# Retention and rational FFN on one core: the value branch of steps 8 to 20 as |b1·h| on ScalarE and one VectorE operation

## The chip, the cores and the metric

The kernel runs on one core of a Trainium2 chip. The metric is the device time of one execution in microseconds (us). Of one execution there is also a profile, which lists every instruction of the engines: TensorE (PE, with its weight loads as PEld), VectorE (DVE), ScalarE (ACT), GpSimd (POOL) and the DMA queues.

## The reference

A retention layer (attention with a decay in place of a softmax) over 8 batches, 8 heads, 576 positions and 64 columns gives 4608 rows of 512. They go through a feed-forward layer of 2048 inner columns whose activation is a ratio of polynomials, element by element:

```
h = x @ w_in
P = a[0] + a[1]*h + a[2]*h**2 + a[3]*h**3
Q = 1 + abs(b[0])*abs(h) + abs(b[1])*h**2
out = (P / (Q + 1e-6)) @ w_out
```

a holds four numbers and b two, and they are known only at run time. Everything is float32.

## The kernel before

**Tiling.** The 4608 rows are nine blocks b of 512 rows, the 2048 inner columns sixteen strips f of 128. A step is one pair (b, f). `gemm1` makes h of a step, a 128x512 tile in PSUM, from 12 matmuls (x and the weights are each split in a high and a low part). The functions `ffn_*` make g = P/Q from it. `gemm2` multiplies g by w_out and adds into the sums of the block, 12 matmuls again. The runs are: steps 0 to 7 (block 0, first half of the strips), steps 8 to 23 (block 1), steps 24 to 31 (block 0, second half), then the other blocks. `gemm2` follows `gemm1` by four steps in steps 8 to 21, by three in most others.

**Early steps.** The weights come from HBM packed as 64-bit words. Until step 23 each strip of weights is loaded and taken apart by `split_weight`: two ScalarE activations (c and bits), one VectorE operation on c, then a ScalarE copy into w and a subtraction on VectorE or GpSimd. `STARTS` says how many splits begin in each step; for steps 8 to 20 it is 0 0 1 1 1 1 1 2 1 0 2 2 1.

**Order.** Each engine gets its instructions in program order (`InOrder`) and runs its queue in that order. In steps 8 to 20 the program order is the list `MID`: start gemm1 split1 ffn_p ffn_hi ffn_r ffn_p2 gemm2 ffn_va ffn_lo split2 ffn_q ffn_v ffn_q3 split3 split0. With i for the step, ScalarE's queue in a step is therefore: c and bits of new splits, p(i) and u(i) from h(i) (`ffn_p`), g(i-2), the logarithm and the exponential that make 1/Q of step i-1 in the tile u (`ffn_r`), v(i) where `VA` says "act" (`ffn_va`), and w of splits that end. VectorE's queue: the operation on c, p·h (`ffn_p`), (p+a1)·h (`ffn_p2`, the last reader of h), v(i) where `VA` says "vector", the two operations of `ffn_q` for step i-1, v·u (`ffn_v`), `ffn_q3` for step i-1, the subtraction of a split.

**Buffers.** h has two PSUM banks (`ps_h`), so gemm1 of step i+2 writes over h(i) and waits for its last reader. In steps 8 to 20 u is not in SBUF but in one of two PSUM banks, `free_at`, which the attention does not need there; from step 21 on it is in SBUF again. v has two buffers, p three. In step 11 the sums of block 0 are taken out of PSUM by two ScalarE copies (o<-acc), and the first `gemm2` of block 1 in step 12 needs the banks that they free.

**The value branch.** Q − (1 + 1e-6) = (|b1|·|h| + |b0|)·|h| is made as u = |h| (ScalarE, in `ffn_p`), v = b1·u + b0 (`ffn_va`: ScalarE or VectorE by the list `VA`), v = v·u (`ffn_v`, VectorE). absb holds |b0| and |b1|, so b0 and b1 in the code are not negative. In steps 8 to 20 `VA` has ScalarE for steps 8, 15 and 16 and VectorE for the ten others.

Of the kernel before, what the change touches and what calls it, by code (L numbers as in the profile page):

```python
# [17 lines left out]
AF = mybir.ActivationFunctionType  # L18
ALU = mybir.AluOpType
# [46 lines left out]
FIRST_DENSE = 22  # L66
SCALES = "scalar pool pool vector pool vector pool scalar pool".split()
SCALES_Q = "vector vector vector pool pool vector vector pool pool".split()
VA = "act act act act vector act act vector act vector vector vector vector vector vector act act vector vector vector vector act act act".split()
LO = "vector pool pool pool pool pool pool pool pool pool pool pool pool vector vector pool pool pool pool pool pool pool vector pool".split()  # L70
WLO = "vector pool pool pool pool pool pool vector vector pool vector vector vector vector pool pool vector vector pool vector pool vector pool vector pool vector pool pool pool pool vector pool".split()
VISITS |= {24 + 2 * i: (8 + i, 9 + i) for i in range(3)}
# [17 lines left out]
def retention_ffn(ctx: ExitStack, tc: tile.TileContext, qkv, w_in, w_out, consts, masks, out):  # L90
# [26 lines left out]
    pe, act, dve, pool = (InOrder(tc, e) for e in (nc.tensor, nc.scalar, nc.vector, nc.gpsimd))  # L117
# [37 lines left out]
    a0, a1, a2, a3 = (ab_sb[:, i : i + 1] for i in range(4))  # L155
    b0, b1 = absb[:, 0:1], absb[:, 1:2]
# [314 lines left out]
    hs = {}  # L471
    els = {}
# [29 lines left out]
        dve.tensor_tensor(p, p, h, ALU.mult)  # L502

    def ffn_p2(b, f):
        p = els[b, f][2]
        dve.scalar_tensor_tensor(p, p, a1, hs.pop((b, f)), ALU.add, ALU.mult)

    def ffn_va(b, f):

        u, v, p = els[b, f]  # L510
        if VA[at[b, f] : at[b, f] + 1] == ["vector"]:
            dve.tensor_scalar(v, u, b1, b0, ALU.mult, ALU.add)
        else:
            act.activation(v, u, AF.Identity, bias=b0, scale=b1)

    def ffn_v(b, f):
        u, v, p = els[b, f]
        dve.tensor_tensor(v, v, u, ALU.mult)

    def ffn_r(b, f):  # L520

# [125 lines left out]
    at = {s[:2]: i for i, s in enumerate(steps)}  # L647
# [84 lines left out]
    for i in range(len(steps) + lag(len(steps))):  # L732
        step = i
        this, prev, prev2 = (steps[j][:2] if 0 <= j < len(steps) else None for j in (i, i - 1, i - 2))
        todo = {"gemm2": (products, i), "start": (split_start, int(STARTS[i]) if i < first else 0)}

        if i in VISITS:
            a, k = VISITS[i]
            todo["visit"] = visit, a, k
            if a is not None:  # L740
                todo |= {f.__name__: (f, a) for f in (keep_hi, keep_lo)}
            if k is not None:
                todo |= {f.__name__: (f, k) for f in ((decay, decay1, add, fade) if a is not None else (decay, add, fade))}
        if i + 1 in VISITS and VISITS[i + 1][1] is not None:
            todo |= {f.__name__: (f, VISITS[i + 1][1]) for f in (scale_q, scale_v)}
        if this:
            todo |= {f.__name__: (f, *this) for f in (gemm1, ffn_p, ffn_p2, ffn_va, ffn_v)}
        if prev:
            todo |= {f.__name__: (f, *prev) for f in (ffn_r, ffn_q, ffn_q3)}
        if prev2:  # L750
            todo |= {"ffn_hi": (ffn_hi, *prev2), "ffn_lo": (ffn_lo, *prev2, i - 2 < first and LO[i - 2] == "pool")}
        if i == half:
            ps = ps_at.tile([P, 2, 512], F32, tag="at", name="free_at")
            free_at.extend((ps[:, 0], ps[:, 1]))
        elif i == FIRST_DENSE - 1:
            free_at.clear()
        whole = i in VISITS
        early = None if half <= i < FIRST_DENSE - 1 or i >= first else (FIRST0, FIRST1, FIRST2, FIRST3, FIRST4, FIRST5, FIRST6, FIRST7, FIRST21, FIRST22, FIRST23)[i if i < half else i - 13]
        dense = DENSE if whole else DENSE_ALONE
        run(END if not this else LAST if i == len(steps) - 1 else MID if free_at else early if i < first else dense if i < 2 * NF else REST, todo)  # L760
        load_weights(2)
# [42 lines left out]
```

## Time and profile before

| | |
|---|---|
| time, median of 3 runs | 869.66 us (868.0 to 869.73) |
| the profiled execution's own time | 868.11 us |
| its span, first to last instruction | 866.0 us |
| PE, DVE, ACT, POOL busy | 98%, 88%, 77%, 15% of the span |
| the chain that ended last, by engine | PE 79%, ACT 10%, DVE 7%, issue 3%, DMA 1% |

The span is what the profile sees; the profiled execution took 2.1 us more than it. A timeline row gives the start of an instruction in us from the span's start, its duration in us, engine, line, operation, output and inputs; in square brackets stands the idle time of the engine just before it and whose end released it. Nearly every instruction is recorded by a helper, line 86, so rows are told apart by their tiles. The steps are told apart by counting h: the h of step 8 is the first whose u goes to free_at.

### The profile page before, as it was taken

The numbers are of one execution on the slowest core, as the hardware profiler recorded it, in microseconds if no ns is written. First come the engines' busy times: TensorE is split into PE (matmuls) and PEld (weight loads), VectorE is DVE, ScalarE is ACT, GpSimd is POOL, SyncE is SP. The second block draws the span as 40 slices with busy tenths as digits, with TensorE's granted clock in tenths as the row PEclk, the third lists the DMA queues.
The fourth block names the chain that finished last, engine by engine and source line by source line (L and its number), as shares of the span: only waits on it lengthen the run. The fifth ranks groups of instructions, "written<-read, shape, count | busy, mean of one in ns | idle before, by whom it ended". The sixth has DMA issues, their size and how long they took to land.

```text
span 866.0 us, 18735 instructions
## 1 busy us (share of the span) xinstructions
PE 845.3 (98%) x7574; PEld 726.4 (84%) x7574; DVE 765.6 (88%) x1221; ACT 669.6 (77%) x1240; POOL 131.2 (15%) x107
## 2 busy tenths in 40 slices
PE   8899899999999999999999999999999999999997
PEld 7667788788888888888888888888888888888886
DVE  5999999999889988898889888888888988888995
ACT  4898999988767778777877787778877787767775
POOL 2522323721001111111111110001111111000000
PEclk9999999999999999999999999999999999999999
DMA  9994000033021112111211121111211121001001
GB/s 345 342 372 178 1 2 0 2 113 116 30 88 50 49 50 98 50 50 50 98 50 51 49 98 51 48 48 31 82 40 50 50 99 50 1 2 48 1 1 48
DMA packets 20774, 64.55 MB, mean 75 GB/s; under 512 B 2512, under 2 KB 2640, under 8 KB 20688
## 3 DMA queue, kind: packets, MB, share of 16 engines
q1 hardware_dynamic: 20528, 63.10, 20.6%
q8 instruction: 59, 0.97, 0.5%
q14 instruction: 27, 0.22, 0.1%
q10 hardware_dynamic: 160, 0.26, 0.1%
HBM read 53.91 MB, written 9.44 MB: 73 GB/s over the span
## 4 chain that ended last, share of the span: by engine, by line
PE 79%; ACT 10%; DVE 7%; issue 3%; DMA 1%; SPq 0%; POOL 0%; POOLq 0%; ACTq 0%; DVEq 0%
PE acc L86 36%; PE h L86 36%; PE ps L86 4%; DVE p L86 3%; PE y L86 2%; DVE v L86 2%; ACT c L86 2%; ACT free_at L86 2%; ACT w L86 1%; ACT p L86 1%; ACT u L86 1%; ACT g L86 1%; DMA qk<-in_qkv 1%; DVE c L86 1%; ACT bits L86 1%
## 5 line engine op out<-in xcount | busy, mean ns | idle before, releaser
L86 PE MATMUL acc<-w,g 128*128 128x512 f32 x1584 | 369.0, 383 | 4.5 <-ACT o L86 2.9
L86 PE MATMUL h<-xhi,w 128*128 128x512 f32 x1152 | 367.2, 381 | 3.6 <-DVE kv L86 1.6
L86 PEld LDWEIGHTS acc<-w,g 128*128 128x128 f32 x1584 | 297.6, 190 | 50.2 <-ACT o L86 3.3
L86 PEld LDWEIGHTS h<-xhi,w 128*128 128x128 f32 x1152 | 217.7, 189 | 37.2 <-ACT c L86 1.7
L86 ACT ACTIVATE p<-h,const_sb 128x512 f32<-128x512 f32 x144 | 111.4, 774 | 161.2 <-PE h L86 154.4
L86 PE MATMUL h<-xlo,w 128*128 128x512 f32 x576 | 218.4, 379 | 0.2 <-DVE xlo L86 0.2
L86 DVE TENSOR_TENSOR p<-p,h 128x512 f32<-128x512 f32 x144 | 98.7, 686 | 47.3 <-ACT u L86 44.9
L86 PEld LDWEIGHTS h<-xlo,w 128*128 128x128 f32 x576 | 108.9, 189 | 16.5 <-issue 0.7
L86 DVE SCALAR_TENSOR_TENSOR p<-p,const_sb,h 128x512 f32<-128x512 f32 x144 | 107.4, 746 | 4.0
L86 ACT ACTIVATE v<-u,absb 128x512 f32<-128x512 f32 x129 | 103.3, 801 | 0.4 <-DVE p L86 0.2
L86 DVE SCALAR_TENSOR_TENSOR p<-v,p 128x512 f32<-128x512 f32 x140 | 98.7, 705 | 3.3
L86 DVE SCALAR_TENSOR_TENSOR p<-p,const_sb,u 128x512 f32<-128x512 f32 x131 | 99.4, 759 | 1.5 <-ACT u L86 1.5
L86 POOL TENSOR_TENSOR S<-S,const_sb 128x256 f32<-128x256 f32 x32 | 32.7, 1022 | 447.6 <-DVE S L86 427.4
L86 DVE TENSOR_TENSOR v<-v,u 128x512 f32<-128x512 f32 x131 | 97.3, 742 | 0.2 <-ACT v L86 0.2
L86 DVE SCALAR_TENSOR_TENSOR v<-v,u 128x512 f32<-128x512 f32 x131 | 89.7, 684 | 0.0
L86 ACT ACTIVATE u<-u 128x512 f32<-128x512 f32 x131 | 82.6, 630 | 4.2
L86 ACT ACTIVATE g<-p 128x512 fp32r<-128x512 f32 x132 | 82.6, 626 | 3.5 <-DVE p L86 3.2
L86 ACT ACTIVATE u<-v 128x512 f32<-128x512 f32 x131 | 81.9, 625 | 1.4 <-DVE v L86 1.4
L86 DVE TENSOR_TENSOR g<-p,g 128x512 fp32r<-128x512 f32 x115 | 78.7, 684 | 0.7 <-ACT g L86 0.7
L86 ACT ACTIVATE u<-h 128x512 f32<-128x512 f32 x131 | 76.8, 586 | 2.0 <-DVE v L86 2.0
L86 ACT ACTIVATE kv<-kv,const_sb 128x64 f32<-128x64 f32 x232 | 58.2, 333 | 4.9 <-DMA kv<-in_qkv 4.9
L86 POOL TENSOR_TENSOR qk<-qk,const_sb 128x512 f32<-128x512 f32 x31 | 44.7, 1442 | 41.0 <-DMA qk<-in_qkv 41.0
(93 smaller groups left out, 699.9 us busy)
## 6 DMA issues: line engine op xcount, KB each, us to landing
qk<-in_qkv SPq DMA_DIRECT2D x36, 512.0 KB, 4.2
kv<-in_qkv SPq DMA_DIRECT2D x32, 512.0 KB, 5.4
bits<-in_w_in SPq DMA_DIRECT2D x16, 512.0 KB, 9.3
bits<-in_w_out SPq DMA_DIRECT2D x16, 512.0 KB, 7.4
out<-o SPq DMA_DIRECT2D x28, 256.0 KB, 3.8
kv<-in_qkv SPq DMA_DIRECT2D x4, 256.0 KB, 6.6
out<-o SPq DMA_DIRECT2D x8, 128.0 KB, 2.1
out<-last SPq DMA_DIRECT2D x2, 256.0 KB, 2.4
```

What stands on the lines that cost most here:

```text
L86: return lambda *a, **k: self.tc.keep_in_program_order(method(*a, **k))
```

## The change

In steps 8 to 20 `VA` now says "abs". There `ffn_p2` also issues, behind its VectorE operation, a ScalarE activation v = |b1·h| that reads h in PSUM; `ffn_va` does nothing; and `ffn_v` is one VectorE operation (v + b0)·u in place of v·u. The list `MID` and all other lists stay as they are.

```diff
-VA = "act act act act vector act act vector act vector vector vector vector vector vector act act vector vector vector vector act act act".split()
+VA = "act act act act vector act act vector abs abs abs abs abs abs abs abs abs abs abs abs abs act act act".split()
     def ffn_p2(b, f):
-        p = els[b, f][2]
-        dve.scalar_tensor_tensor(p, p, a1, hs.pop((b, f)), ALU.add, ALU.mult)
+        u, v, p = els[b, f]
+        h = hs.pop((b, f))
+        dve.scalar_tensor_tensor(p, p, a1, h, ALU.add, ALU.mult)
+        if VA[at[b, f] : at[b, f] + 1] == ["abs"]:
+            act.activation(v, h, AF.Abs, scale=b1)
     def ffn_va(b, f):
         u, v, p = els[b, f]
+        if VA[at[b, f] : at[b, f] + 1] == ["abs"]:
+            return
     def ffn_v(b, f):
         u, v, p = els[b, f]
-        dve.tensor_tensor(v, v, u, ALU.mult)
+        if VA[at[b, f] : at[b, f] + 1] == ["abs"]:
+            dve.scalar_tensor_tensor(v, v, b0, u, ALU.add, ALU.mult)
+        else:
+            dve.tensor_tensor(v, v, u, ALU.mult)
```

## Rows read from the trace of the kernel before

**Rows 1.** The page, part 1: busy time of each engine over the span.
```profile
PE 845.3 (98%) x7574; PEld 726.4 (84%) x7574; DVE 765.6 (88%) x1221; ACT 669.6 (77%) x1240; POOL 131.2 (15%) x107
```

**Rows 2.** Busy time by stretch; columns us, PE, PEld, DVE, ACT, POOL, clock, DMA.
```profile
80.00:160.00 80.00, 75.11 (x337) 64.08 (x335) 77.17 (x120) 76.36 (x121) 26.44 (x20) 0.98 0.00 1
160.00:190.00 30.00, 29.17 (x395) 24.30 (x394) 29.83 (x43) 26.68 (x55) 15.29 (x12) 1.00 0.16 53
190.00:240.00 50.00, 50.00 (x570) 43.50 (x569) 45.89 (x79) 40.46 (x83) 5.58 (x6) 1.00 0.28 94
```

**Rows 3.** Timeline of PE, 97 to 163 us: first matmuls behind its waits.
```profile
100.71 4.54 PE L86 MATMUL acc<-w,g 128*128 128x512 f32 x12 [2.90 <-ACT o L86]
...
112.86 2.75 PE L86 MATMUL acc<-w,g 128*128 128x512 f32 x12
...
147.75 0.48 PE L86 MATMUL h<-xhi,w 128*128 128x512 f32 x1 [0.64 <-DVE p L86]
...
154.40 0.45 PE L86 MATMUL h<-xhi,w 128*128 128x512 f32 x1 [1.20 <-ACT free_at L86]
...
157.06 5.73 PE L86 MATMUL acc<-w,g 128*128 128x512 f32 x24
```

**Rows 4.** Instructions by form, 80 to 160 us: count, busy us, mean ns, idle.
```profile
L86 ACT ACTIVATE p<-h,const_sb 128x512 f32<-128x512 f32 x14 | 10.7, 766 | 0.0
...
L86 DVE SCALAR_TENSOR_TENSOR p<-p,const_sb,free_at 128x512 f32<-128x512 f32 x13 | 9.6, 739 | 0.4 <-ACT v L86 0.3
...
L86 DVE TENSOR_TENSOR v<-v,free_at 128x512 f32<-128x512 f32 x13 | 8.8, 680 | 0.0
...
L86 DVE TENSOR_SCALAR v<-free_at,absb 128x512 f32<-128x512 f32 x10 | 8.1, 807 | 0.4
...
L86 ACT ACTIVATE free_at<-h 128x512 f32<-128x512 f32 x13 | 7.7, 589 | 0.8 <-DVE v L86 0.8
```

**Rows 5.** Timeline of ACT, 84 to 155 us, steps 8 to 20.
```profile
84.04 0.77 ACT L86 ACTIVATE v<-free_at,absb 128x512 f32<-128x512 f32 x1
84.71 0.86 ACT L86 ACTIVATE w<-held 128x512 fp32r<-128x512 f32 x1
...
88.40 0.89 ACT L86 ACTIVATE w<-held 128x512 fp32r<-128x512 f32 x1
...
105.57 0.58 ACT L86 ACTIVATE free_at<-free_at 128x512 f32<-128x512 f32 x1
106.07 0.62 ACT L86 ACTIVATE w<-c 128x512 fp32r<-128x512 f32 x1
...
114.64 0.58 ACT L86 ACTIVATE free_at<-h 128x512 f32<-128x512 f32 x1 [0.52 <-DVE v L86]
...
132.30 0.58 ACT L86 ACTIVATE free_at<-h 128x512 f32<-128x512 f32 x1 [0.30 <-DVE v L86]
133.27 0.64 ACT L86 ACTIVATE g<-p 128x512 fp32r<-128x512 f32 x1 [0.39 <-DVE p L86]
...
134.91 0.62 ACT L86 ACTIVATE w<-c 128x512 fp32r<-128x512 f32 x1
...
154.19 1.14 ACT L86 ACTIVATE w<-c 128x512 fp32r<-128x512 f32 x2
```

**Rows 6.** Timeline of DVE, 88 to 136 us: the two operations on h.
```profile
88.72 0.75 DVE L86 SCALAR_TENSOR_TENSOR p<-p,const_sb,h 128x512 f32<-128x512 f32 x1
...
104.61 0.69 DVE L86 TENSOR_TENSOR p<-p,h 128x512 f32<-128x512 f32 x1 [0.30 <-ACT free_at L86]
105.34 0.75 DVE L86 SCALAR_TENSOR_TENSOR p<-p,const_sb,h 128x512 f32<-128x512 f32 x1
...
135.07 0.75 DVE L86 SCALAR_TENSOR_TENSOR p<-p,const_sb,h 128x512 f32<-128x512 f32 x1
```

**Rows 7.** All waits, summed by pair: us in total, times, longest.
```profile
DVE p L86 <- ACT u L86: 46.4, 82, 1.7
```

**Rows 8.** Busy time and granted clock in short stretches; columns as in rows 2.
```profile
101.00:104.00 3.00, 3.00 (x8) 2.34 (x8) 3.00 (x6) 2.97 (x6) 0.00 (x0) 0.50 0.00 0
...
152.00:155.00 3.00, 1.80 (x9) 1.30 (x8) 2.90 (x5) 2.97 (x7) 1.38 (x2) 1.00 0.00 0
```

## The prediction

> **What bounds the kernel now.** The page comes first: PE is busy for 98% of the span, and no other engine comes near it [rows 1]. So only what makes PE stand still can move the time. The busy time by stretch tells where it does [rows 2]. From 190 us on PE has no gap worth naming (50.00 of 50 in the stretch shown), so a delay that PE has at 190 us is a delay of the end, us for us. Between 80 and 160 us, which holds steps 8 to 20, PE idles 4.89 us, and there both other engines are nearly full: VectorE idles 2.83 us of the 80 and ScalarE 3.64. The change moves work between just these two, in just this stretch.
>
> PE's timeline shows where its gaps lie [rows 3]. Step 12 loses 2.90 us because the two ScalarE copies that empty the sums of block 0 come late; then the matmuls of steps 21 and 22 wait 0.64 and 1.20 us for their bank of h. A step of PE needs 2.59 us for each of its two sets (twelve matmuls take 2.75 with a tail of 0.16), 5.18 in all. ScalarE needs about as much for a step with one split and more with two, so PE runs ahead until it lacks a bank. From 154.40 on, where the h of step 22 starts, PE sets the pace. **The question is thus when that matmul starts.**
>
> One more view matters: who may read h when. In step 12 VectorE's p·h starts at 104.61 after 0.30 of idle [rows 6]. Of its inputs p had long been written; what had just ended is u, which ScalarE also reads from h. Over the whole run VectorE loses 46.4 us in 82 such waits [rows 7]. So two engines do not read one bank of h at a time here: the later one in program order waits. The Trainium skill (PSUM — Partial Sum Buffer, "PSUM bank collisions raise a hardware error") says that reads of one bank by two engines collide, and that semaphores have to keep them apart; the trace agrees with these 46.4 us.
>
> **The change part by part.** VectorE, in ten steps, loses an operation of 0.807 us; in thirteen, v·u of 0.680 becomes a two-scalar-and-tensor form, for which the nearest row has 0.739 [rows 4]. That is 10 × 0.807 − 13 × 0.059 = 7.3 us less for VectorE.
>
> ScalarE gets ten more activations. None that reads h with a scale from a tile and no bias is in the trace. From below it is bounded by u, 0.589, with neither, from above by p, 0.766, with both [rows 4]; it has one of the two, so I take the middle, 0.68. The next instruction starts 0.10 before such a one ends (84.04 + 0.77 against 84.71) [rows 5], so its place in the queue costs 0.58 (bounds 0.49 and 0.67). In steps 8, 15 and 16 it replaces one of 0.67 and saves 0.09.
>
> The Trainium skill (ScalarE: Activation LUTs, "Rules for kernel authors") speaks against this trade: additions and products belong on VectorE, which it calls up to three times as fast. It says so of bf16, and no row here has that form; by that ratio an operation of 0.807 would cost 2.4 us on ScalarE, an estimate, and ten of them some 18 us more than in my sum. The rows of float32 from PSUM have 0.807 against at most 0.766, so the trade is one for one.
>
> The second part is a **new wait**. The activation reads h behind (p+a1)·h in program order, so ScalarE now waits for VectorE to end that. Behind it on ScalarE stand w, the next split's c and bits and then p and u of the next step, for which VectorE and, through the bank, PE wait. How long it is depends on how late VectorE is:
> - Step 12, the common case: ScalarE would be free at 106.07, VectorE is done at 105.34 + 0.75, and 0.04 passes between dependent instructions [rows 5, 6]: 0.06 us.
> - Step 9: ScalarE would be free at 88.40, VectorE only ends at 88.72 + 0.75 = 89.47, with the longer v·u of step 8 at 89.53. The activation starts at 89.57 and ScalarE goes on at 90.15. VectorE has no relief before, since step 8 had its value branch on ScalarE already.
> - Step 17: ScalarE free at 134.91, VectorE done at 135.07 + 0.75. That is 0.95; VectorE loses some 0.25 of its lag in the steps ahead, so I take 0.70. Here too steps 15 and 16 bring VectorE no relief.
>
> The lag of ScalarE's queue against before, summed up:
> - behind step 9: 90.15 − 88.40 = 1.75 (step 8's saving is in it)
> - steps 10 to 14: 5 × (0.58 + 0.06) = 3.20; the 0.52 that it idled in step 14 for VectorE [rows 5] goes: 4.43
> - steps 15 and 16: 2 × (0.06 − 0.09): 4.37
> - step 17: 0.58 + 0.70: 5.65
> - steps 18 to 20: 3 × 0.64 = 1.92: 7.57.
>
> The copies out of the sums in step 11 are late with it, by some 3 us, so the gap of 2.90 grows. That does not count twice: behind it PE again runs ahead of ScalarE. The activation of step 20 is now the last reader of its h. It stands just ahead of the w at 154.19 [rows 5], so it starts at 154.19 + 7.57 − 0.58 = 161.18, ends at 161.86, and the h of step 22 starts at 161.90 and not at 154.40: **7.5 us late**.
>
> What comes back behind it: the 24 matmuls at 157.06 took 5.73 [rows 3]; at 0.215 each and the length of one, 0.38, they need 23 × 0.215 + 0.38 = 5.33. The 0.4 is a wait in the middle for g's low part, which is no longer late when PE is: 7.1. Of the 0.83 that PE idles between 160 and 190 [rows 2], where VectorE is full, I give back 0.2, as VectorE comes there a little less late than PE. That leaves **6.9 us**.
>
> The profiled execution took 868.1 us, so the sum is 875.0. The median of the runs is 1.5 above that execution; from it the sum would be 876.6. I name the middle, 875.8. By the bounds of the activation alone (10 × 0.09 each way) it is 874.9 to 876.7.
>
> **The rivals.**
> - *No wait between the two readers of h.* If VectorE and ScalarE may read h together, the 1.17 of step 9, the 0.70 of step 17 and the 0.06s go, and with them the idle 0.30 and 0.39 of step 17 [rows 5] that ScalarE could fill. The lag behind step 20 is 10 × 0.58 − 3 × 0.09 − 0.52 − 0.69 = 4.3, and after the same 0.6 comes back 3.7: 871.8 to 873.4. Rows 7 speak against it.
> - *The clock falls at the new gaps.* After the 2.90 gap the clock stood at 1.2 of 2.4 GHz, 0.50 from 101 to 104 us, and the twelve matmuls took 4.54 for 2.75; over the gap of 1.20 it stayed at 1.00 [rows 3, 8]. Steps 20 to 22 now have gaps of some 2 us each, in between. If it falls at step 22, 1.8 us more are lost where nothing hides them: 877.6. It decides from a gap somewhere between 1.20 and 2.90.
> - *VectorE was the bound, and this is faster.* By the busy time it is a little fuller than ScalarE [rows 2], and the gaps of 0.64 and 1.20 end with a VectorE operation on h. If its 7.3 us of relief are what counts, both gaps go: 868.1 − 1.8 = 866.3, on the median 867.8. The Trainium skill (VectorE: DVE Perf Modes, "Rules for kernel authors") has it that VectorE's operation count is what to bring down, and by that rule this is the result. It decides if the new activation fits in ScalarE's idle time, 3.64 over ten, 0.36 us each. The cheapest reader of h takes 0.49 of its queue, so I think little of it.
> - *Hidden.* ScalarE's lag could be made up by waits that I count as staying, within 0.2% (1.7 us).
>
> **How the numbers follow.** Forecast 0.63, no wait 0.14, clock 0.11, faster 0.07, hidden 0.05. About 0.2% is what a measurement of this kernel can tell from no change. The first three are slower by more than that: 0.88. The range leaves out faster and hidden, starts at the no-wait case from the profiled time, 871.8, and ends at the clock case with the dear activation, counted from the median, 879.
>
> **What would show it.** ScalarE rows v<-h,absb, thirteen, of 0.59 to 0.77 us; no TENSOR_SCALAR on free_at; a wait of ScalarE's v for VectorE's p of about 1 us in steps 9 and 17 and of a few hundredths elsewhere; ScalarE over 98% busy or waiting in the stretch and VectorE with some 7 us more idle; the copies out of the sums near 102.5; the first matmul of step 22 near 162, and from there the same timeline. I am wrong if ScalarE's v starts while VectorE still reads h, if its other activations get shorter when VectorE does less, or if PE starts step 22 before 157.

## The result, and the profile after

The kernel after takes 875.13 us (median of 4 runs, 874.57 to 876.18); the kernel before, run beside it, took 869.59 (4 runs, 868.00 to 869.73). The ratio of the runs is 1.0076 [1.0064, 1.0089], some 6.6 us slower; the two medians lie 5.5 us apart. The forecast was 875.8, between 871.8 and 879.0. The profiled execution of after took 875.41 us with a span of 873.3; that of before took 868.11 with 866.0.

The page, part 1, of after (busy time of each engine, its share of the span, instructions), beside [rows 1]:
```profile
PE 847.7 (97%) x7574; PEld 727.4 (83%) x7574; DVE 762.7 (87%) x1211; ACT 675.8 (77%) x1250; POOL 132.9 (15%) x107
```
VectorE lost 2.9 us of work and ScalarE got 6.2, and the time followed neither share: on the page both engines look three quarters or more full, as before. Where the time went stands in the busy time by stretch, beside [rows 2]; after's stretches are cut 7 us later, so that they hold the same work (us, PE, PEld, DVE, ACT, POOL, clock, DMA):
```profile
80.00:160.00 80.00, 71.57 (x311) 59.91 (x310) 68.23 (x100) 75.25 (x120) 21.62 (x16) 0.96 0.00 1
160.00:167.00 7.00, 5.26 (x25) 4.28 (x24) 6.76 (x9) 6.91 (x14) 4.98 (x4) 1.00 0.01 2
167.00:197.00 30.00, 29.55 (x397) 24.89 (x396) 29.82 (x43) 26.87 (x54) 15.60 (x12) 1.00 0.16 51
197.00:247.00 50.00, 50.00 (x570) 43.50 (x569) 45.91 (x79) 40.78 (x84) 5.57 (x6) 1.00 0.27 93
```
From 167 us on, PE's busy time is within 0.4 us of what it was from 160 us on before, stretch by stretch. All that was lost is lost ahead of that. VectorE now idles 12 us of the first 80 instead of 3, while ScalarE idles 5 instead of 4.

PE's timeline, 97 to 171 us, beside [rows 3] (start, us, what, and in brackets the idle time before it with its releaser):
```profile
103.83 5.49 PE L86 MATMUL acc<-w,g 128*128 128x512 f32 x12 [3.84 <-ACT o L86]
...
141.12 0.48 PE L86 MATMUL h<-xhi,w 128*128 128x512 f32 x1 [0.61 <-ACT v L86]
...
148.47 0.48 PE L86 MATMUL h<-xhi,w 128*128 128x512 f32 x1 [1.90 <-ACT v L86]
...
155.16 0.48 PE L86 MATMUL h<-xhi,w 128*128 128x512 f32 x1 [1.25 <-ACT v L86]
...
162.35 0.48 PE L86 MATMUL h<-xhi,w 128*128 128x512 f32 x1 [1.74 <-ACT v L86]
...
165.04 5.34 PE L86 MATMUL acc<-w,g 128*128 128x512 f32 x24
```
The h of step 22 starts at 162.35 instead of 154.40. The releaser of all four waits for h is now the new activation v: it has become the last reader of the bank. The 24 matmuls behind it take 5.34 where they took 5.73.

Of those 7.95 us, 0.50 was there before the change begins. That shows in ScalarE's p of step 8, the first operation on the h of that step. In the ScalarE timeline of before it stands at
```profile
81.16 0.76 ACT L86 ACTIVATE p<-h,const_sb 128x512 f32<-128x512 f32 x1
```
and in that of after, with the waits that matter beside [rows 5]:
```profile
81.66 0.76 ACT L86 ACTIVATE p<-h,const_sb 128x512 f32<-128x512 f32 x1
...
90.07 0.69 ACT L86 ACTIVATE v<-h,absb 128x512 f32<-128x512 f32 x1 [1.01 <-DVE p L86]
...
102.76 1.93 ACT L86 ACTIVATE o<-acc 128x1024 f32<-128x1024 f32 x2
...
128.38 0.69 ACT L86 ACTIVATE v<-h,absb 128x512 f32<-128x512 f32 x1 [0.33 <-DVE p L86]
...
137.80 0.63 ACT L86 ACTIVATE g<-p 128x512 fp32r<-128x512 f32 x1 [0.57 <-DVE p L86]
...
140.38 0.69 ACT L86 ACTIVATE v<-h,absb 128x512 f32<-128x512 f32 x1 [0.85 <-DVE p L86]
...
161.61 0.69 ACT L86 ACTIVATE v<-h,absb 128x512 f32<-128x512 f32 x1
```
So each kernel is best measured by one stretch, **from step 8's p to the first matmul of step 22**: 73.24 us before, 80.69 after, 7.45 more. What follows that matmul took 711.6 us of the span before and 710.95 after. It was between 710.95 and 713.4 in every kernel below, so this stretch carries nearly all of the difference, but for e1 and e8 to e10, where up to 1.8 us more is lost behind it.

The two VectorE operations that the waits of 1.01 and 0.85 end with, beside [rows 6]:
```profile
89.29 0.75 DVE L86 SCALAR_TENSOR_TENSOR p<-p,const_sb,h 128x512 f32<-128x512 f32 x1
...
139.60 0.75 DVE L86 SCALAR_TENSOR_TENSOR p<-p,const_sb,h 128x512 f32<-128x512 f32 x1
```
89.29 + 0.75 = 90.04, and v starts at 90.07; 139.60 + 0.75 = 140.35, and v starts at 140.38. The two readers of one bank do follow each other.

The forms, 80 to 167 us, beside [rows 4] (count, busy us, mean ns, idle before them):
```profile
L86 DVE SCALAR_TENSOR_TENSOR p<-v,p 128x512 f32<-128x512 f32 x14 | 12.1, 867 | 0.0
...
L86 DVE SCALAR_TENSOR_TENSOR v<-v,absb,free_at 128x512 f32<-128x512 f32 x13 | 9.6, 742 | 0.0
L86 DVE TENSOR_TENSOR p<-p,h 128x512 f32<-128x512 f32 x14 | 9.6, 688 | 10.2 <-ACT free_at L86 10.2
...
L86 ACT ACTIVATE v<-h,absb 128x512 f32<-128x512 f32 x13 | 8.9, 687 | 2.2 <-DVE p L86 2.2
```
The new activation takes 0.687 us (0.68 forecast), the new VectorE operation 0.742 (0.739). VectorE now waits 10.2 us for ScalarE ahead of p·h, 1.4 before: what it was relieved of became waiting for the engine that was given more.

### The profile page after: what moved, and what is told of

The parts are those of the page before. It is cut to its first block, busy times and chain, and to the rows that moved or that the text cites. A ratio compares the mean times of both kernels' runs of the same rounds, so it can differ in the third digit from the quotient of the medians.

```text
span 873.3 us, 18733 instructions
## 1 busy us (share of the span) xinstructions
PE 847.7 (97%) x7574; PEld 727.4 (83%) x7574; DVE 762.7 (87%) x1211; ACT 675.8 (77%) x1250; POOL 132.9 (15%) x107
## 4 chain that ended last, share of the span: by engine, by line
PE 76%; DVE 3%; ACT 2%; issue 0%; POOL 0%; SPq 0%; POOLq 0%; ACTq 0%
PE acc L86 36%; PE h L86 34%; PE ps L86 4%; PE y L86 2%; DVE p L86 1%; DVE v L86 1%; ACT free_at L86 0%; DVE c L86 0%; ACT g L86 0%; ACT p L86 0%; ACT kv L86 0%; ACT c L86 0%; ACT w L86 0%; POOL g L86 0%; DVE qk L86 0%
## 5 line engine op out<-in xcount | busy, mean ns | idle before, releaser
L86 POOL TENSOR_TENSOR S<-S,const_sb 128x256 f32<-128x256 f32 x32 | 35.7, 1116 | 448.8 <-DVE S L86 425.1
L86 POOL TENSOR_TENSOR qk<-qk,const_sb 128x512 f32<-128x512 f32 x31 | 42.4, 1368 | 38.9 <-DMA qk<-in_qkv 38.9
```

Of the source, the lines that this page charges most:

```text
L86: return lambda *a, **k: self.tc.keep_in_program_order(method(*a, **k))
```

## The experiments

The theory is that ScalarE's queue is what the stretch goes by, and that ten activations and ScalarE's new wait for VectorE are paid there in full. The rivals are that VectorE set the pace, that the place of the activation is what costs, and that the idle times of ScalarE are slack to be filled. All figures of the stretch are the one defined above, less 73.24, and come from one profiled execution each; the two timing columns are medians and ratios to the kernel before, run beside each.

| kernel | stretch, us | span, us | time, us | ratio |
|---|---|---|---|---|
| before | 0 | 866.0 | 868.48 to 869.59 | 1 |
| after: all of 8 to 20 | +7.45 | 873.3 | 875.13 | 1.0076 [1.0064, 1.0089] |
| e3_abs_three: 8, 15, 16 | +0.08 | 866.0 | 868.08 | 0.9995 [0.9984, 1.0006] |
| e5_abs_9_11: 9 to 11 | +2.80 | 868.7 | 871.63 | 1.0035 [1.0023, 1.0046] |
| e6_abs_17_20: 17 to 20 | +2.81 | 868.3 | 871.64 | 1.0035 [1.0022, 1.0048] |
| e11_abs_9: step 9 | +1.34 | 867.7 | 869.82 | 1.0012 [1.0003, 1.0021] |
| e12_abs_18: step 18 | +0.61 | 867.3 | 869.21 | 1.0002 [0.9990, 1.0015] |
| e4_vector_less | −0.87 | 865.3 | 867.50 | 0.9990 [0.9978, 1.0002] |
| e7_scalar_less | +1.39 | 867.7 | 870.07 | 1.0013 [1.0003, 1.0022] |
| e1_act_all | +6.10 | 873.3 | 875.21 | 1.0080 [1.0065, 1.0095] |
| e2_abs_early | +5.48 | 871.5 | 874.03 | 1.0069 [1.0054, 1.0084] |
| e8_w_vector | +7.76 | 876.5 | 875.66 | 1.0072 [1.0055, 1.0089] |
| e9_early_w_vector | +5.00 | 872.5 | 874.34 | 1.0067 [1.0045, 1.0089] |
| e10_before_w_vector | +5.10 | 873.2 | 875.25 | 1.0073 [1.0054, 1.0093] |

### Is it VectorE? The product left out

```diff
     def ffn_v(b, f):
         u, v, p = els[b, f]
+        if at[b, f] in (9, 10, 11, 12, 13, 14, 17, 18, 19, 20):
+            return
         dve.tensor_tensor(v, v, u, ALU.mult)
```


> Edit: from the kernel before, the ten steps with the branch on VectorE leave out the product v*u, so VectorE has 10 x 0.60 us less of its queue and ScalarE nothing more (Q lacks a factor |h| there). Queue theory: ScalarE sets the pace; it gets back at most its idle time for VectorE, 0.52 in step 14 and 0.69 in step 17, so 0.5 to 1.6 us faster than before. Rival, VectorE is the bound of the stretch: the gaps of PE at steps 21 and 22 go and more, 2 to 6 us faster.

VectorE's busy time on the page falls by 5.4 us (765.6 to 760.2), more than the 2.9 of the change, and ScalarE is given nothing: the stretch shortens by 0.87 us, the span by 0.7, and the time by an amount that its interval does not set apart from none. PE's gap at step 22 in this run:
```profile
153.66 0.45 PE L86 MATMUL h<-xhi,w 128*128 128x512 f32 x1 [1.16 <-ACT free_at L86]
```
The gap of 1.20 is 1.16, with the same releaser. The rival "VectorE was the bound" falls. The rule put beside it, that VectorE's operation count is what to bring down (Trainium skill, VectorE: DVE Perf Modes, "Rules for kernel authors"), does not give the time here: ten operations less shortened the stretch by 0.87 us.

### Is it ScalarE? Three activations less

```diff
-        if VA[at[b, f] : at[b, f] + 1] == ["vector"]:
+        if VA[at[b, f] : at[b, f] + 1] == ["vector"] or at[b, f] in (8, 15, 16):
             dve.tensor_scalar(v, u, b1, b0, ALU.mult, ALU.add)
...
     def ffn_v(b, f):
         u, v, p = els[b, f]
+        if at[b, f] in (8, 15, 16):
+            return
```


> Edit: from the kernel before, steps 8, 15 and 16 make v = b1*u + b0 on VectorE in the place of the product v*u, which is left out there (Q lacks a factor |h| in three steps). ScalarE has 3 x 0.67 = 2.0 us less of its queue, VectorE 3 x 0.13 more. Queue theory: what comes off ScalarE comes off the end, as far as VectorE does not become late: 1.0 to 2.0 us faster than before, with a third of the work that the run with less VectorE work took away for 0.7 us of span. Rival, both engines are equally the pace: 0.4 us slower to 0.3 faster.

A miss: 1 to 2 us less were expected, and the stretch is 1.39 longer. ScalarE lost 2.0 us of work and got waits in their place. Its timeline in steps 9 and 17:
```profile
86.96 0.63 ACT L86 ACTIVATE g<-p 128x512 fp32r<-128x512 f32 x1 [0.69 <-DVE p L86]
...
133.11 0.78 ACT L86 ACTIVATE p<-h,const_sb 128x512 f32<-128x512 f32 x1 [1.99 <-DVE g L86]
```
and what VectorE did until the second:
```profile
131.53 1.49 DVE L86 TENSOR_TENSOR g<-p,g 128x512 fp32r<-128x512 f32 x1
```
In step 9 the 0.64 that ScalarE had gained in step 8 is gone at once: g waits for VectorE's p and starts 5.59 us behind step 8's p, just where it does in before. In step 17, 131.53 + 1.49 = 133.02. p has three buffers, and this p waits for the low part of an earlier g, which VectorE makes from the buffer's old p. The edit put an operation of 0.81 ahead of that g, and 0.81 of the 1.49 is GpSimd holding VectorE up (see the last section; 0.68 is usual), so the 1.39 is not the price of this relief alone. But ScalarE is not the one bound either. The two engines wait for each other in turn (p and u from ScalarE to VectorE, buffers and g's input from VectorE to ScalarE), and both are near their limit in these steps. Relief of either alone brought little in e4 and nothing here.

### The same trade without the new activation

```diff
-VA = "act act act act vector act act vector act vector vector vector vector vector vector act act vector vector vector vector act act act".split()
+VA = "act act act act vector act act vector act act act act act act act act act act act act act act act act".split()
```


> Edit: from the kernel before, v = b1*u + b0 goes to ScalarE in all of steps 8 to 20 (ten more activations that read u and not h; v*u stays). VectorE is relieved as in the change, ScalarE gets as much work (0.67 of its queue each instead of 0.58), but no activation waits for VectorE's last operation on h. Queue theory (the lag of ScalarE's queue, work plus waits, is the loss): 10 x 0.67 less 0.5 to 1.2 of idle time that goes, so a lag of 5.5 to 6.2 behind step 20, of which the h of step 22 sees that of p of step 20, 4.8 to 5.5, and some 0.6 comes back: 4.2 to 4.9 us over the kernel before, and 2 us less than the change. Rival 1, the wait for VectorE costs nothing: as slow as the change or slower by 10 x 0.09, +6.5 to +7.5. Rival 2, VectorE is the bound: faster than before by 1 to 2 us.

Here v = b1·u + b0 is on ScalarE in all thirteen steps, behind u and not behind VectorE. The stretch is 6.10 longer, more than the 4.8 to 5.5 expected at that matmul, and the time is that of after, not 2 us less. The number is that of the rival "the wait costs nothing"; the rows show another sum. Such an activation lasts 0.77 to 0.78 us and takes 0.67 or more of the queue (146.47 to the next at 147.15), ten of them 6.7. Of ScalarE's idle times only that of step 14 went (0.52); those of step 17 stayed:
```profile
136.24 0.58 ACT L86 ACTIVATE free_at<-h 128x512 f32<-128x512 f32 x1 [0.31 <-DVE v L86]
...
137.20 0.63 ACT L86 ACTIVATE g<-p 128x512 fp32r<-128x512 f32 x1 [0.38 <-DVE p L86]
```
Behind step 22, PE loses another 0.95:
```profile
167.62 2.43 PE L86 MATMUL acc<-w,g 128*128 128x512 f32 x10 [0.95 <-POOL g L86]
```
This is the split low part of g, late on GpSimd. So e1 ends where after does by dearer activations and a late g, but with no new wait for h. Whether that wait costs anything, e11 and e12 below tell.

### The steps one group at a time

All of these have the new code of `ffn_p2`, `ffn_va` and `ffn_v`, and differ in `VA` alone. e3 has "abs" in steps 8, 15 and 16, where it replaces an activation by a cheaper one:
```diff
+VA = "act act act act vector act act vector abs vector vector vector vector vector vector abs abs vector vector vector vector act act act".split()
```


> Edit: the new form only in steps 8, 15 and 16, where the branch was on ScalarE already; the ten others as before. Queue theory: ScalarE saves 3 x 0.09 and may wait 0.1 to 0.3 in step 16, VectorE pays 3 x 0.06: no change that can be measured, -0.5 to +0.6 us. Rival, the new form itself is dear (its reading of h late holds the bank): slower by 1 us or more.

No change, as expected, in stretch, span and time. Where ScalarE gets no more work, the new wait and the change of form cost nothing that is seen. (Some 0.4 us of this stretch is the clock's, which stayed high behind the gap of step 12; see the rival on the clock below.)

e5 has it in steps 9 to 11, all other entries of `VA` as before:


> Edit: the new form only in steps 9, 10 and 11, ahead of the copies out of the sums; all other steps as before. Queue theory: the lag adds up step by step wherever it arises and PE's running ahead does not swallow it. Behind step 11 it is 1.75 + 2 x 0.64 = 3.0; of it 0.52 (step 14) and up to 0.69 (step 17) of idle time is filled; h of step 22 1.8 to 2.5 late, up to 0.4 comes back: +1.4 to +2.3 us over the kernel before. Rival, only the last steps count, since PE and ScalarE find each other again after the gap at step 12: 0 us. Rival, the later copies cost their full lag: +3 us, with PE's low clock perhaps more.

2.80 us later at the h of step 22, above the 1.8 to 2.5 that were expected there: none of ScalarE's idle time was filled. ScalarE's timeline:
```profile
89.39 0.69 ACT L86 ACTIVATE v<-h,absb 128x512 f32<-128x512 f32 x1 [1.01 <-DVE p L86]
...
117.52 0.58 ACT L86 ACTIVATE free_at<-h 128x512 f32<-128x512 f32 x1 [0.53 <-DVE v L86]
...
135.20 0.58 ACT L86 ACTIVATE free_at<-h 128x512 f32<-128x512 f32 x1 [0.31 <-DVE v L86]
136.16 0.63 ACT L86 ACTIVATE g<-p 128x512 fp32r<-128x512 f32 x1 [0.38 <-DVE p L86]
```
The last three are the 0.52, 0.30 and 0.39 of before [rows 5], some 2.9 us later and not shorter. **ScalarE came 2.9 us late to a wait of 0.53, and the wait was still there.** VectorE, which it waits for, had been waiting for ScalarE and was as late itself. Its p·h of step 12, beside [rows 6]:
```profile
107.48 0.69 DVE L86 TENSOR_TENSOR p<-p,h 128x512 f32<-128x512 f32 x1 [1.63 <-ACT free_at L86]
```
That is 2.87 later than in before, and from there VectorE has no idle time up to the v that ends the 0.53. More work on ScalarE did not fill this idle time; in e4, where VectorE came earlier, that of step 14 was gone (those of step 17 stayed). Of the 2.80, some 0.4 is not the edit's, as in e3.

e6 has it in steps 17 to 20:


> Edit: the new form only in steps 17 to 20; all other steps as before. Queue theory: step 17 gives 0.58 and a wait of 0.95, steps 18 to 20 3 x 0.64, a lag of 3.4 behind step 20; the activation of step 20 as last reader of h lets h of step 22 start 3.4 late, 0.6 comes back: +2.6 to +3.0 us over the kernel before. Rival, only the last steps count: nearly all of the change's loss, +5 or more. Rival, VectorE's relief in these steps ends PE's gaps at steps 21 and 22: 0 or faster.

2.81 us later at the h of step 22, for the 3.4 expected there; the span is 2.3 longer, for 2.6 to 3.0. ScalarE's timeline has the wait of step 17 in full, though VectorE was relieved in none of the steps ahead:
```profile
136.01 0.69 ACT L86 ACTIVATE v<-h,absb 128x512 f32<-128x512 f32 x1 [0.85 <-DVE p L86]
```
and PE shows what comes back when the new activation of step 20 is the last reader of h: 5.34 for the 24 matmuls, and 710.95 us from the h of step 22 to the end, as in after:
```profile
157.35 0.48 PE L86 MATMUL h<-xhi,w 128*128 128x512 f32 x1 [0.95 <-ACT v L86]
...
160.05 5.34 PE L86 MATMUL acc<-w,g 128*128 128x512 f32 x24
```
Behind step 17 ScalarE's queue is 1.57 late, as in after. Steps 18 to 20 then add 1.30, where in after they add 1.92. The difference is step 18, whose split operations were some 0.6 us shorter while the granted clock was low (the rival on the clock and the last section have the rows). So this number is smaller than forecast for a reason that the edit did not make.

With the 0.08 of e3, the stretches of e5 and e6 add up to 5.69 of the 7.45. No run has steps 12 to 14 alone; in after's timeline the lag grows by 1.27 over them. With the clock's share in e3, e5 and e6 the sum is good to some half a us.

e11 has it in step 9 alone, e12 in step 18 alone: the same instructions added and removed, once where VectorE is late and once where it is not.

> Edit: the new form in step 9 alone, where VectorE ends its last operation on h some 1.0 us after ScalarE would be free. One activation more. If the wait counts like work: 0.58 + 1.0 = 1.6 us over the kernel before at the first matmul of step 22 and at the end, although VectorE has 0.75 less. Rival, only the work counts: 0.6 us. Rival, so early a lag is swallowed by step 12's gap: 0.

> Edit: the new form in step 18 alone, where VectorE is done with h when ScalarE is free. One activation more. If the wait counts like work: 0.6 us over the kernel before, since there is next to none here. Rival, each activation costs the same wherever it stands: the same as the form in step 9 alone, 1.1 to 1.6. Rival, VectorE's 0.75 less shortens the gaps at steps 21 and 22: 0 or faster.

ScalarE's timeline of e11, then of e12:
```profile
89.78 0.69 ACT L86 ACTIVATE v<-h,absb 128x512 f32<-128x512 f32 x1 [1.00 <-DVE p L86]
```
```profile
142.34 0.69 ACT L86 ACTIVATE v<-h,absb 128x512 f32<-128x512 f32 x1
```
1.34, for 1.6 expected, against 0.61. The 0.61 is the 0.58 that the activation takes of the queue, and hardly more. In step 9 most of the wait of 1.00 comes on top. By the times e12 can't be told from before and e11 only just (0.3 to 1.8 us); the stretches in the traces are what decides.

### The activation elsewhere

```diff
     def ffn_p(b, f):
...
+        if VA[at[b, f] : at[b, f] + 1] == ["abs"]:
+            act.activation(v, h, AF.Abs, scale=b1)
...
     def ffn_p2(b, f):
...
-        if VA[at[b, f] : at[b, f] + 1] == ["abs"]:
-            act.activation(v, h, AF.Abs, scale=b1)
```


> Edit: from the change, the activation v = |b1*h| is issued in ffn_p right behind u, ahead of VectorE's first operation on h, so ScalarE never waits for VectorE there and VectorE's p*h comes 0.58 later instead. Queue theory: the waits of steps 9, 16 and 17 (2.2 us in the changed kernel's rows) and the 0.05 of each other step go; lag behind step 20 of 4.4 to 5.0; h of step 22 now waits for VectorE's last operation on h, 0.5 later behind p than before: 4.4 to 4.9 late, 3.8 to 4.3 us over the kernel before, 2.5 to 3 less than the change. Rival 1, the wait costs nothing because PE or VectorE would be late anyway: as slow as the change, +6 to +7. Rival 2, moving the reader ahead makes VectorE late by 0.58 in every step and the loss stays the same by that way: +6 or more with ScalarE idle for VectorE in g and in the logarithm.

Here the activation stands right behind u, so ScalarE reads h three times in a row and VectorE after it. 5.48 us, 2 less than after and more than expected. The waits of 1.01 and 0.85 are gone from v, and stand elsewhere in ScalarE's timeline:
```profile
86.70 0.58 ACT L86 ACTIVATE free_at<-h 128x512 f32<-128x512 f32 x1 [0.68 <-DVE v L86]
...
135.67 0.58 ACT L86 ACTIVATE free_at<-h 128x512 f32<-128x512 f32 x1 [1.06 <-DVE v L86]
```
The second was 0.30 in before, with a further 0.39 behind it that is gone here. VectorE is late in these two steps here too, and ScalarE meets it at the next thing that it needs. By the times, the intervals of e2 and after overlap (1.0054 to 1.0084 and 1.0064 to 1.0089): the stretch is shorter, and that the time is, is not shown.

### Work handed back to VectorE

If ScalarE has too much and VectorE now has room, a ScalarE operation that VectorE can do should pay. The copy that ends a split is one:
```diff
-        act.activation(halved[0], cf, AF.Copy)
+        if 9 <= step <= 20 and not late:
+            dve.tensor_copy(halved[0], cf)
+        else:
+            act.activation(halved[0], cf, AF.Copy)
```
e8 does it on the kernel after, e9 on e2, e10 on before.

> Edit: from the change, the copy of a split's high part (w<-c, thirteen in steps 9 to 20, 0.52 of ScalarE's queue each) goes to VectorE. ScalarE has 6.8 us less than in the change, VectorE 13 copies of 0.35 to 0.60 more, 4.5 to 7.8 against the 7.3 that the change took from it. Queue theory: the new form was slower because its work landed on the engine that sets the pace; paid back with other work of that engine most of the loss goes: 4 to 7 us less than the change, -1 to +3 us against the kernel before. Rival, the wait for VectorE's operation on h is what costs: it gets longer with a fuller VectorE, and the loss stays above +4 us.

> Edit: the early activation (issued behind u, ahead of VectorE's operations on h) and the copies w<-c of steps 9 to 20 on VectorE. Queue theory: as in the run with the copies on VectorE alone, without the waits of steps 9, 16 and 17 in ScalarE but with VectorE's operations on h 0.58 later: -1.5 to +2 us against the kernel before, and less than that run by 0 to 1.5. Rival: VectorE, now full, is the pace, and its delay by 0.58 per step costs more than the waits: slower than that run.

> Edit: from the kernel before, only the copies w<-c of steps 9 to 20 on VectorE. ScalarE has 6.8 us less, VectorE 4.5 to 7.8 more, of which its idle time in the stretch holds 2.8. Queue theory: now VectorE sets the pace: 1 to 5 us slower than before, so that the gain of the two runs above is owed to both moves together. Rival: ScalarE was the pace by so much that its relief wins: faster than before by 1 us or more.

All three are some 6 us slower than before; e8 and e9 were expected near it, e10 1 to 5 us slower. ScalarE's timeline of e8:
```profile
159.17 0.88 ACT L86 ACTIVATE c<-bits 128x512 f32<-128x512 f32 x1 [3.83 <-POOL w L86]
```
This wait is 0.87 in before and in after. It is for GpSimd's subtraction of a split, which frees the buffer that c is to fill. GpSimd's timeline of e8:
```profile
157.75 1.39 POOL L86 TENSOR_TENSOR w<-c,w 128x512 fp32r<-128x512 f32 x1 [2.81 <-DVE w L86]
```
The copy, in VectorE's queue, comes behind VectorE's work on h, and GpSimd waits 2.81 us for it. In e9 the wait of c is 4.48 and in e10 5.37. The copies were cheap on VectorE (13 of 0.42 us in e8); in this step it is their place that cost. That is not the whole loss: in e8 the waits of v for VectorE's work on h are 3.5 us in all, 2.2 in after, as the rival there had it, and in e10 VectorE is busy for 78.06 of the 80 us from 80 to 160, and ScalarE waits 2.62 and 2.12 us for it in two places. Whether another order of step 20 would keep the gain was not tried and stays open. (e8's time is from its other runs: its profiled execution, 878.55, is the longest of its four.)

No kernel here beats before: the intervals of e3 and e4 take in 1, and e4 leaves work out.

## Why the prediction was right

**The sign and the mechanism** are as predicted: work moved one for one from VectorE to ScalarE, a new wait of ScalarE for VectorE, the activation of step 20 as the last reader of h, and the h of step 22 late, with PE full behind it.

**The lag of ScalarE's queue**, read as the start of the next step's p counted from step 8's p, after less before:

| behind step | 9 | 14 | 16 | 17 | 20 |
|---|---|---|---|---|---|
| predicted, us | 1.75 | 4.43 | 4.37 | 5.65 | 7.57 |
| measured, us | 1.63 | 3.90 | 4.02 | 5.59 | 7.51 |

The last entry fits to 0.06 partly by luck: the misses on the way, −0.12, −0.41, +0.18 and +0.29, cancel.

- *Step 9:* a wait of 1.01 and a lag of 1.63, for 1.17 and 1.75. e11 has it by itself: 1.34 to the matmul, of which 0.61 is the bare activation by e12.
- *Steps 10 to 14:* 2.27 where 2.68 was predicted. The idle 0.52 of step 14 did go in after, though e5 shows that lag alone doesn't remove it.
- *Steps 15 and 16:* +0.12 for −0.06. There was a wait that I did not see, 0.33 in step 16, at 128.38.
- *Step 17:* +1.57 for +1.28. The wait was 0.85 for 0.70: the relief that VectorE has in the steps ahead changed nothing, as e6 shows with the same 0.85 and none. ScalarE's two idle times there stayed in sum: u starts 0.89 behind p (1.06 in before) and g 1.15 behind u (0.97).
- *Steps 18 to 20:* 1.92, as predicted.
- *h of step 22:* 7.45 late for 7.5.

**What comes back:** 0.65 (711.6 less 710.95) for 0.6, and the 24 matmuls took 5.34 for 5.33.

**The sum.** 7.45 − 0.65 = 6.8, for 6.9. The spans differ by 7.3, as the stretch ahead of step 8 was 0.50 longer in this execution; nothing shows that the change did this, and over the kernels above step 8's p lies between 81.05 and 83.44.

**The term that was off** is the last one: I named the middle between the sum from the profiled execution, 875.0, and that from the median, 876.6. The median came out at 875.13, so the 0.8 for half of that offset was not there. In the later series before's median was 868.48 twice, 869.35 and 869.25, of 13 to 23 runs, 0.4 to 1.2 above the profiled execution's 868.11, and after's median lies 0.3 below its own profiled execution: the offset of 1.5, from a median of three, is not one to carry over.

**VectorE's relief** was put at 7.3 us, and its busy time fell by 2.9. The two operations cost what was predicted; what I left out is that others got longer. Of the 4.4 us between, p<-v,p has 14 × (0.867 − 0.739) = 1.8 (see the last section). That did not decide the time, by e4.

**The rivals.**
- *No wait between the readers:* refuted by the starts at 90.07 and 140.38. Its lag of 4.3 us was too low as well: it counted ScalarE's idle times as room, and in e2, where v does not wait for VectorE, the stretch is 5.48.
- *The clock falls at the new gaps:* at step 22 it did not. The gaps of 1.90, 1.25 and 1.74 left it at 1.00. Busy time and granted clock in short stretches of after, beside [rows 8]:
```profile
103.00:106.00 3.00, 2.17 (x5) 1.81 (x6) 2.60 (x5) 2.97 (x5) 0.00 (x0) 0.50 0.00 0
...
162.00:163.00 1.00, 0.65 (x3) 0.60 (x4) 1.00 (x3) 1.00 (x3) 0.11 (x1) 1.00 0.00 0
```
It fell where it had before, at the gap of step 12, which grew from 2.90 to 3.84; the twelve matmuls took 5.49 for 4.54. The copies ended that gap 2.6 us later than in before, counted from step 8's p (some 3 were predicted), but PE came to it later too. Behind that PE waits for banks of h again, from 141.12 on, for an engine that the slow matmuls did not hold up.

As far as these runs show, it is luck that the clock held at step 22. The prediction took the length of the gap to decide, somewhere between 1.20 and 2.90, and it does not. In e6 a gap of 1.89, as long as the 1.90 of after and ahead of the same h, is followed by a granted clock of 0.50 (PE's timeline, then the stretch behind it):
```profile
144.09 0.48 PE L86 MATMUL h<-xhi,w 128*128 128x512 f32 x1 [1.89 <-ACT v L86]
```
```profile
145.00:146.00 1.00, 1.00 (x4) 0.79 (x3) 1.00 (x3) 0.97 (x3) 0.00 (x0) 0.50 0.00 0
```
In e3 and e5, gaps of 2.74 and 3.84 at step 12 left the clock at 1.00, and the twelve matmuls took 2.86. PE's timeline of e3, then of e5:
```profile
100.64 2.86 PE L86 MATMUL acc<-w,g 128*128 128x512 f32 x12 [2.74 <-ACT o L86]
```
```profile
103.14 2.86 PE L86 MATMUL acc<-w,g 128*128 128x512 f32 x12 [3.84 <-ACT o L86]
```
What decides it stays open. In e9 and e10 it did fall at step 22, behind gaps of 3.98 and 3.75, and what follows that matmul took 1.2 and 1.8 us longer than in before, other waits included. Where ScalarE set the pace, as at step 20 of e6, the low clock did not cost: it made ScalarE's split operations shorter (last section), 0.6 us in e6. In before and after these operations take 0.68 to 0.69 behind the gap of step 12, in e3 and e5 0.88 to 0.91, which is the 0.4 us named there; the comparison of before and after is free of it.
- *VectorE the bound:* refuted by e4. *Hidden:* refuted by the time; e5 shows that ScalarE's waits do not make its lag up.
- *The rule of the dear activation* (Trainium skill, ScalarE: Activation LUTs, "Rules for kernel authors") is for bf16; taken over, it would have had 2.4 us for each, an estimate. In float32 from PSUM it took 0.687, less than the 0.807 that it replaced on VectorE.

## What to carry to other kernels

Where two engines hand tiles to each other in turn, a one-for-one trade between them was paid in full here on the one that takes the work, and hardly repaid on the other: find the start that sets the end (here the first matmul of step 22) and count the queue of the engine that feeds it. An added reader of a PSUM bank also adds a wait for the reader ahead of it, worth most where that engine is late (1.34 against 0.61 us for the same edit in two steps), and it may become the last reader that the next matmul waits for. An engine's idle time that ends with an engine which waits for it in turn is not room: here it moved along with 2.9 us of lag and stayed as long as it was. And differences of half a us between single executions need a look at the granted clock, which can differ behind the same gap.

## What was unexpected of the hardware

**VectorE held up by GpSimd.** p<-v,p took 0.69 us in most steps and up to 1.29 in some, and in after there are more of the long ones. In step 17 GpSimd's row, and VectorE's:
```profile
135.94 1.28 POOL L86 TENSOR_TENSOR w<-c,w 128x512 fp32r<-128x512 f32 x1 [4.97 <-ACT w L86]
```
```profile
136.53 1.23 DVE L86 SCALAR_TENSOR_TENSOR p<-v,p 128x512 f32<-128x512 f32 x1
```
GpSimd ends at 137.22, VectorE at 137.76, 0.54 later. The other long ones of after end 0.54 to 0.55 behind a GpSimd operation too, and e7's g<-p,g of 1.49 is 0.55 behind one. The Trainium skill (SBUF — State Buffer, "SBUF: two separate sides") says that a VectorE operation with two inputs in SBUF takes a pair of ports that GpSimd shares, and that whoever starts first keeps it for the whole instruction; these rows agree for a GpSimd operation that started first. The late g at 137.80 in after follows directly from it.

**ScalarE's split operations are shorter when TensorE runs slowly or stands.** In e6, behind the gap that ends at 144.09, they take 0.67 to 0.68, where before has 0.82 to 0.88 in the same step. PE is busy all that time, at a granted clock of 0.50 (the stretch from 145 to 146 us shown above). ScalarE's timeline of e6:
```profile
144.72 0.68 ACT L86 ACTIVATE bits<-bits 128x512 int32<-128x512 uint32 x1
145.30 0.67 ACT L86 ACTIVATE c<-bits 128x512 f32<-128x512 f32 x1
```
and of before:
```profile
142.44 0.87 ACT L86 ACTIVATE bits<-bits 128x512 int32<-128x512 uint32 x1
143.20 0.86 ACT L86 ACTIVATE c<-bits 128x512 f32<-128x512 f32 x1
```
In e10 the one at 138.35 takes 0.67 while PE stands in a gap of 0.99. The slow stretch thus gave back some 0.6 us of ScalarE's queue in e6. Why was not tried.
